# Stage one of a Fourier mixing kernel: two half-width weight tiles in place of two zero-padded full-width ones

## The chip, the cores and the metric

The kernel runs on one core of a Trainium2 chip. A core has a matrix engine (TensorE, PE in the profile; its weight loads are listed apart as PEld), a vector engine (VectorE, DVE), an activation engine (ScalarE, ACT), a general engine (GpSimd, POOL) and a queue engine (SyncE, SP), each with an instruction queue of its own, and 16 DMA engines. The metric is the time of one execution on the device, in microseconds (us); lower is better.

## The reference

The input `x` holds 8 batches of 3072 x 256 numbers. The result is the real part of a Fourier transform over the 3072 positions and the 256 features of each batch, followed by a feed-forward layer that takes the largest of three products:

```python
def _attn_ref(x) -> np.ndarray:
    X = np.fft.fft(x, axis=1)
    X = np.fft.fft(X, axis=2)
    return X.real.astype(np.float32)

def _moe_ref(x, w1, w2, w3, w_out) -> np.ndarray:
    h = np.maximum(np.maximum(x @ w1, x @ w2), x @ w3)
    return (h @ w_out).astype(np.float32)
```

The output is 24576 x 256 in float32.

## The kernel before

The transform over 3072 positions is done as 32 x 96. For each batch a `Mix` object (L358 and on) has these steps: `s(k)` for k = 0 to 6 is stage one, `y` writes its result to DRAM in another order, `z` reads it back into `yb`, `u` and `x0` make the column of feature 0 apart, `c` puts that column into `yb`, `k` is the second stage, which gives the even and odd halves `tE` and `tO`, `v` spreads one row over all partitions, and `end` takes the middle position. The transform over the features is folded into the weights: `gE`, `gO`, `gD` stand for the products of the transform's matrix with w1, w2, w3, and `gw` for the part that passes straight to the output.

Stage one multiplies `x` by a table of 64 columns (32 angles, cosine and sine) over 128 partitions. It has 49 positions `s` of 128 features. Positions of even `s` go to the upper 64 partitions of the result `tb`, those of odd `s` to the lower 64. One call `s(k)` for k under 6 takes eight positions: four even ones as the 512 columns of one matmul, four odd ones as those of another, and both add up in one bank `ps1` of 128 x 512 in float32. The weights of both are 128 columns wide. The tile `tabz` (L93) has 192 columns, of which the middle 64 hold the table and the rest zeros; `tab_at[0]` is its columns 64 to 191 (table, then zeros), `tab_at[1]` its columns 0 to 127 (zeros, then table). So the first matmul writes the even positions to the upper half and zeros to the lower, and the second adds zeros to the upper half and the odd positions to the lower. `s(6)` is the last position alone: one matmul of 128 columns (L375), of which only 64 partitions are read. An eviction (a copy by ACT, in batch 1 for two of them by DVE) then takes the bank to `tb` (L373, L377).

The table itself is made once at the start, by DVE from the sines that ACT gives (L224 to L226).

The main part runs over 8 batches x 18 units (`UNITS`, three blocks of 512 positions x six columns of 128 hidden features). A unit's `begin` and `finish` do the products of the first layer (L437, L438, L445, and for odd units L756, L758, L772, L773, whose third product goes over ACT, DVE and POOL in `third`), and `l2_some` puts ten steps of the second layer (L461, L476, L484) among them. The next batch's `Mix` steps are put between units by a table written out by hand, `ahead` (L729 to L734): the order on each engine's queue is fixed by it.

```python
    ahead = {1: ("s0", "s1"), 2: ("s2", "y0", "s3"), 3: ("u", "s4", "s5"), 4: ("s6", "y1", "x"),
             7: ("z",), 11: ("c",), 12: ("kO0",), 13: ("v0", "kE0", "kO1"), 14: ("v1", "kE1"),
             15: ("kO2",), 16: ("v2", "kE2", "end")}
```

So for batches 2 to 7 PE meets three groups of four stage-one matmuls (units 1, 2 and 3) and then that of `s(6)` alone (unit 4), which `x0` follows (L400): two matmuls with 98 columns of weights that POOL copies in `u` (L395). In batch 0 all is done at the start in two groups (L599 to L608), with idle matmuls (`warm_up`, L589) ahead of each; in batch 1 there are three groups. `ps1` comes from a pool of three banks (`ps_f`, L79) that `k`, `third`, `l2_block` and others share; in batch 0 from one of five (`ps_s`).

In the last batch `l2_mid` (L535) does the middle positions of all batches: among its matmuls are eight whose weights have only 8 columns (L555, L461).

Of the kernel before, what the change touches and what calls it, by code (L numbers as in the profile page):

```python
# [10 lines left out]
BF16 = mybir.dt.bfloat16  # L11
INT32 = mybir.dt.int32
AX = mybir.ActivationFunctionType
ALU = mybir.AluOpType
# [36 lines left out]
def kernel(  # L51
# [9 lines left out]
    nc = tc.nc  # L61
# [16 lines left out]
    consts = ctx.enter_context(tc.tile_pool(name="consts", bufs=1))  # L78
# [11 lines left out]
    x0s = consts.tile([128, RI], BF16, tag="x0s")  # L90
    x0u = consts.tile([128, KS + 1], BF16, tag="x0u")
    ybv = yb.rearrange("p (r e f) -> p r e f", e=2, f=128)
    tabz = consts.tile([128, 192], BF16, tag="tabz")  # L93
    tab_at = [tabz[:, 64:192], tabz[:, 0:128]]
    tabx = consts.tile([128, 2 * RI], BF16, tag="tabx")
    te_tab = consts.tile([128, NHALF + 1], BF16, tag="te_tab")
    to_tab = consts.tile([128, NHALF + 1], BF16, tag="to_tab")
# [20 lines left out]
    def load_x(b, s0, s1, h):  # L118

        rows = x[b].rearrange("(a s) d -> a s d", s=96)  # L120
        lo, hi = (s0, s1) if h == 0 else (max(s0, 1), min(s1, 48))
        src = rows[:, lo:hi, :] if h == 0 else rows[:, 97 - hi:97 - lo, :][:, ::-1, :]
        return nc.gpsimd.dma_start(out=xt[b % 2][32 * h:32 * h + 32, lo:hi, :], in_=src)
# [75 lines left out]
    def small(name):  # L199
        return gen.tile([128, 1], FP32, name=name, tag=name)  # L200

    def scal(out, in0, s1, op0, s2=None, op1=None, eng=None):
        kw = {} if op1 is None else {"op1": op1}
        return (eng or nc.vector).tensor_scalar(out=out, in0=in0, scalar1=s1, scalar2=s2,
                                                op0=op0, **kw)

    up, sidx, hflag, alpha, sig, sgm = (small(n) for n in
                                        ("up", "sidx", "hflag", "alpha", "sig", "sgm"))
# [10 lines left out]
    ang_q = gen.tile([128, 4 * RI], FP32, tag="ang_q")  # L219
# [1 line left out]
                                   op0=ALU.mult, op1=ALU.add)  # L221
    _reduce(nc, ang_r, ang_r, ang_q, 32.0)
    nc.scalar.activation(out=ang_q, in_=ang_r, func=AX.Sin, scale=float(2.0 * math.pi / 32.0))
    nc.vector.memset(tabz, 0.0)  # L224
    nc.vector.tensor_copy(out=tabz[:, 64:128:2], in_=ang_q[:, 0:32])
    scal(tabz[:, 65:128:2], ang_q[:, 0:32], sig, ALU.mult)  # L226
    scal(tabx, ang_q[:, 2 * RI:4 * RI], sgm, ALU.mult)

    dve = nc.vector.tensor_copy
# [8 lines left out]
    for fc in range(2):  # L238
        scal(pf[:, fc:fc + 1], pidx, float(128 * fc), ALU.add)
        nc.vector.scalar_tensor_tensor(  # L240
            out=vm[:, fc * 256:(fc + 1) * 256].rearrange("p (k c) -> p k c", c=128),
# [14 lines left out]
                          in_=par.unsqueeze(1).to_broadcast([128, 2, 2]))  # L256
# [101 lines left out]
    class Mix:  # L358
# [8 lines left out]
        def s(self, k, pool=ps_f, evict=nc.scalar.copy):  # L367
            ps1 = pool.tile([128, 512], FP32, name="ps1", tag="ps")
            if k < 6:
                for hh in range(2):  # L370
                    nc.tensor.matmul(ps1, tab_at[hh], self.x[:, 8 * k + hh:8 * k + 8:2, 0:128],  # L371
                                     start=(hh == 0), stop=(hh == 1))
                evict(out=tb[:, k * 512:(k + 1) * 512], in_=ps1)  # L373
            else:
                nc.tensor.matmul(ps1[:, 0:128], tab_at[0], self.x[:, 48, 0:128],  # L375
                                 start=True, stop=True)
                evict(out=tbv[0:64, 24, :], in_=ps1[0:64, 0:128])  # L377

        def y(self, s0=0, s1=NS, second=nc.sync):
# [241 lines left out]
    for (s0, s1) in HALVES:  # L621
        for h in range(2):
            load_x(1, s0, s1, h)
        if s0 == 0:
            nc.gpsimd.dma_start(out=wout_bf.rearrange("p (jc c) -> p jc c", jc=NJC),
                                in_=moe_w_out.rearrange("(jc p) c -> p jc c", jc=NJC))
# [235 lines left out]
```

## Time and profile before

The median of the runs is 408.67 us. The page and the trace come from one profiled execution with its own time.

| | |
|---|---|
| runs before, us | 408.67, 407.83, 408.88 |
| the profiled execution | 407.28 us |
| its span, first to last instruction | 405.5 us |
| granted TensorE clock, mean | 0.993 |
| matmuls of L371 (512 columns) | 96, 379 ns each from start to modelled end |
| matmuls of L375 (128 columns) | 8, 219 ns each |
| evictions L373 by ACT | 46, 586 ns (median) |
| evictions L373 by DVE | 2, 692 ns |
| evictions L377 by ACT (64 x 128) | 8, 258 ns (median) |

A line of a group names the source line, the engine, the operation, output and inputs with the weights' and the moving tile's sizes, then the count, the busy time in us and the mean in ns of one, and the idle time of the engine just before. A matmul's duration runs to a modelled end, and the next one starts before that: what a matmul costs PE's queue is the distance from its start to the next start, which the timeline shows. A timeline line is the start and the length of a stretch, what ran in it and how many, and in square brackets the idle time before it with what ended it. The chain of waits is followed back from the last instruction, at each step to what released it.

### The profile page before, as it was taken

What the parts mean: (1) busy time and instruction counts of PE and PEld (TensorE: products, weight loads), DVE (VectorE), ACT (ScalarE), POOL (GpSimd) and SP (SyncE); (2) the same over time, 40 slices, a digit from 0 to 9 for tenths busy, and PEclk for the clock granted to TensorE, in tenths of its full rate; (3) what the DMA queues carried; (4) which work ended last, traced back from release to release, by engine and by line L of the source; (5) the groups of instructions that cost most, each with busy time, mean ns of one, the idle gap of its engine ahead of it and who ended that gap; (6) DMA issues with size and microseconds to landing.
All of it is one profiled execution on the core that took longest, in us unless ns stands there. A gap on an engine that the chain in (4) does not pass through costs nothing.

```text
span 405.5 us, 8306 instructions
## 1 busy us (share of the span) xinstructions
PE 388.1 (96%) x2695; PEld 242.7 (60%) x2743; DVE 319.3 (79%) x543; ACT 262.8 (65%) x466; POOL 322.1 (79%) x403
## 2 busy tenths in 40 slices
PE   8689899999999999999999999999999999999995
PEld 3245466656666566656665666656666656666574
DVE  7869787867887887867887887867887887887982
ACT  2565779768866778568875778567875546635430
POOL 7376469878989799888988799887988699788991
PEclk9899999999999999999999999999999999999999
DMA  8999967495765858394765958395532553322225
GB/s 126 195 167 186 187 192 139 127 171 143 162 151 105 178 156 164 107 169 116 188 158 107 180 146 163 114 163 129 150 106 78 145 142 99 96 66 69 88 81 142
DMA packets 69692, 56.30 MB, mean 139 GB/s; under 512 B 35040, under 2 KB 65248, under 8 KB 68452
## 3 DMA queue, kind: packets, MB, share of 16 engines
q0 software_dynamic: 23376, 26.27, 35.0%
q1 hardware_dynamic: 45106, 28.86, 27.3%
q10 hardware_dynamic: 1168, 0.65, 0.6%
q8 instruction: 21, 0.34, 0.3%
q14 instruction: 21, 0.17, 0.2%
HBM read 38.15 MB, written 31.71 MB: 172 GB/s over the span
## 4 chain that ended last, share of the span: by engine, by line
PE 70%; DMA 11%; DVE 5%; issue 4%; ACT 4%; POOL 4%; SPq 1%; ACTq 0%; DVEq 0%; POOLq 0%
PE po L461 24%; PE pse L445 10%; PE pse L437 7%; DMA out_dram<-ot 7%; PE pse L438 5%; PE pse L772 3%; PE po L484 3%; PE d L758 3%; PE pse L773 3%; PE e L756 3%; PE ps L412 2%; DVE even L761 2%; DMA yb<-db 2%; PE pl L476 2%; POOL minus L765 2%
## 5 line engine op out<-in xcount | busy, mean ns | idle before, releaser
L451 ACT ACTIVATE stmp<-pse 128x512 bf16<-128x512 f32 x150 | 89.6, 598 | 61.7 <-PE pse L445 46.4
L765 POOL TENSOR_TENSOR plus<-even,odd 128x512 bf16<-128x512 f32 x69 | 87.9, 1273 | 41.2 <-DVE even L761 35.0
L571 POOL DMA_INDIRECT out_dram<-ot,rows_m x92 | 102.4, 1113 | 17.8 <-issue 9.3
L765 POOL TENSOR_TENSOR minus<-even,odd 128x512 bf16<-128x512 f32 x69 | 87.6, 1270 | 0.0
L774 DVE SCALAR_TENSOR_TENSOR hp<-pse,plus 128x512 bf16<-128x512 f32 x69 | 47.6, 690 | 49.8 <-PE pse L773 21.3
L461 PE MATMUL po<-wout_bf,hp 128*128 128x256 bf16 x576 | 86.1, 273 | 0.3
L461 PE MATMUL po<-wout_bf,hm 128*128 128x256 bf16 x576 | 78.6, 273 | 0.0
L461 PEld LDWEIGHTS <-hp 128*128 128x128 bf16 x576 | 56.3, 98 | 26.1
L445 PE MATMUL pse<-tO,gD 128*128 128x512 bf16 x218 | 70.6, 378 | 0.7
L461 PEld LDWEIGHTS <-hm 128*128 128x128 bf16 x576 | 56.3, 98 | 16.4
L489 DVE TENSOR_TENSOR ot<-po,even 128x512 f32<-128x512 f32 x92 | 62.7, 682 | 0.0
L452 DVE TENSOR_TENSOR hp<-pse,stmp 128x512 bf16<-128x512 f32 x75 | 51.4, 685 | 10.9 <-ACT stmp L451 9.3
L437 PE MATMUL pse<-tE,gE 128*128 128x512 bf16 x147 | 55.6, 378 | 1.5 <-ACT stmp L451 0.2
L452 DVE TENSOR_TENSOR hm<-pse,stmp 128x512 bf16<-128x512 f32 x75 | 51.6, 688 | 6.4 <-ACT stmp L451 2.7
L761 DVE SCALAR_TENSOR_TENSOR even<-vb,wcol,e 128x512 f32<-128x512 bf16 x69 | 50.9, 737 | 0.0
L786 DVE SCALAR_TENSOR_TENSOR hm<-pse,minus 128x512 bf16<-128x512 f32 x69 | 47.1, 682 | 3.6 <-PE pse L445 3.4
L438 PE MATMUL pse<-tO,gO 128*128 128x512 bf16 x130 | 49.2, 379 | 0.6 <-ACT tO L414 0.4
L760 ACT ACTIVATE odd<-d 128x512 f32<-128x512 f32 x69 | 41.3, 598 | 6.7
L130 ACT COPY xt<-xt 64x762 bf16<-64x762 bf16 (+1 forms) x48 | 40.2, 838 | 1.1
L373 ACT CAST tb<-ps 128x512 bf16<-128x512 f32 x46 | 24.8, 589 | 23.2 <-PE ps L371 23.1
L445 PEld LDWEIGHTS <-gD 128*128 128x128 bf16 x219 | 21.2, 97 | 20.3 <-issue 0.7
L484 PE MATMUL po<-gw,tO 128*128 128x512 bf16 x86 | 32.7, 380 | 0.0
(156 smaller groups left out, 475.1 us busy)
## 6 DMA issues: line engine op xcount, KB each, us to landing
yb<-db SPq DMA_DIRECT2D x7, 833.0 KB
xt<-in_x_dram POOLq DMA_DIRECT2D x14, 384.0 KB, 6.2
out_dram<-ot SPq DMA_DIRECT2D x56, 96.0 KB
out_dram<-ot SPq DMA_DIRECT2D x64, 64.0 KB
db<-tb SPq DMA_DIRECT2D x21, 192.0 KB
vb<-vd SPq DMA_DIRECT2D x23, 128.0 KB
xt<-in_x_dram POOLq DMA_DIRECT2D x7, 400.0 KB, 6.1
xt<-in_x_dram POOLq DMA_DIRECT2D x7, 368.0 KB, 5.9
```

The costliest lines, as they stand in the source:

```text
L437: nc.tensor.matmul(pse[:, 0:n], gE[i][:, js], te, start=True, stop=False)
L438: nc.tensor.matmul(pse[:, 0:n], gO[i][:, js], to, start=False, stop=True)
L445: nc.tensor.matmul(pse, gD[i][:, js], to, start=False, stop=True, skip_group_check=True)
L451: nc.scalar.activation(out=stmp[:, 0:n], in_=pses[0][:, 0:n], func=AX.Relu)
L452: nc.vector.tensor_tensor(out=dst, in0=src3, in1=stmp[:, 0:n], op=ALU.max)
L461: nc.tensor.matmul(po, hcols(jc), wout_bf[:, jc * 256:(jc + 1) * 256], start=False, stop=(jc == NJC - 1), skip_group_check=True)
L489: nc.vector.tensor_tensor(out=ot.rearrange("p (h c) -> p h c", h=2), in0=po.rearrange("p (h c) -> p h c", h=2), in1=lin.unsqueeze(1).to_br ...
L571: stored(nc.gpsimd.indirect_dma_start(out, bass.IndirectOffsetOnAxis(ap=rows_m[0:128 - lo, at_row: at_row + 1], axis=0), ot[lo:128, 256:51 ...
L761: nc.vector.scalar_tensor_tensor(out=even3, in0=vb, scalar=wcol[:, jc:jc + 1], in1=e3, op0=ALU.mult, op1=ALU.add)
L765: nc.gpsimd.tensor_tensor(out=dst, in0=even3, in1=odd3, op=op)
L774: nc.vector.scalar_tensor_tensor(out=dst, in0=pse2, scalar=0.0, in1=sums[g][0], op0=ALU.max, op1=ALU.max)
L786: nc.vector.scalar_tensor_tensor(out=dst, in0=pses[0], scalar=0.0, in1=sums.pop(g)[1], op0=ALU.max, op1=ALU.max)
```

## The change

The table loses its zeros. It is now `tab`, 64 columns wide, and each matmul of stage one has 64 columns of weights and an output of 64 partitions: partitions 0 to 63 of the bank for the even positions, at column position 0 of the array, and 64 to 127 for the odd ones, at column position 64. Each of the two is a group of its own (start and stop), since nothing is added up any more. `s(6)` uses column position 0 alone. The evictions are as before. The memset of `tabz` is gone.

```diff
-    tabz = consts.tile([128, 192], BF16, tag="tabz")
-    tab_at = [tabz[:, 64:192], tabz[:, 0:128]]
+    tab = consts.tile([128, 64], BF16, tag="tab")
...
-    nc.vector.memset(tabz, 0.0)
-    nc.vector.tensor_copy(out=tabz[:, 64:128:2], in_=ang_q[:, 0:32])
-    scal(tabz[:, 65:128:2], ang_q[:, 0:32], sig, ALU.mult)
+    nc.vector.tensor_copy(out=tab[:, 0:64:2], in_=ang_q[:, 0:32])
+    scal(tab[:, 1:64:2], ang_q[:, 0:32], sig, ALU.mult)
...
                 for hh in range(2):
-                    nc.tensor.matmul(ps1, tab_at[hh], self.x[:, 8 * k + hh:8 * k + 8:2, 0:128],
-                                     start=(hh == 0), stop=(hh == 1))
+                    nc.tensor.matmul(ps1[hh * 64:hh * 64 + 64], tab,
+                                     self.x[:, 8 * k + hh:8 * k + 8:2, 0:128],
+                                     start=True, stop=True, tile_position=(0, 64 * hh))
                 evict(out=tb[:, k * 512:(k + 1) * 512], in_=ps1)
             else:
-                nc.tensor.matmul(ps1[:, 0:128], tab_at[0], self.x[:, 48, 0:128],
-                                 start=True, stop=True)
+                nc.tensor.matmul(ps1[0:64, 0:128], tab, self.x[:, 48, 0:128],
+                                 start=True, stop=True, tile_position=(0, 0))
                 evict(out=tbv[0:64, 24, :], in_=ps1[0:64, 0:128])
```

## The prediction

> **What bounds the kernel now.** I read the page's busy shares and chain first, then the windows of two whole batches, then the places on TensorE (PE) that the change touches.
>
> ```profile
> PE 388.1 (96%) x2695; PEld 242.7 (60%) x2743; DVE 319.3 (79%) x543; ACT 262.8 (65%) x466; POOL 322.1 (79%) x403
> ...
> PE 70%; DMA 11%; DVE 5%; issue 4%; ACT 4%; POOL 4%; SPq 1%; ACTq 0%; DVEq 0%; POOLq 0%
> ```
> ```profile
> 79.47:125.34 45.87, 45.46 (x320) 28.78 (x324) 36.66 (x58) 33.47 (x58) 39.30 (x48) 1.00 0.68 148
> 125.34:171.20 45.86, 45.45 (x321) 28.79 (x324) 36.58 (x58) 33.47 (x58) 39.56 (x48) 1.00 0.67 149
> ```
>
> The windows' columns are the stretch, its length, then busy time of PE, PEld (weight loads), DVE, ACT, POOL, the granted clock, DMA share and GB/s. In a steady batch of 45.9 us PE is idle for 0.4 us, at full clock; the next, POOL, has some 6 us free. So a microsecond of PE's queue is a microsecond of time there, unless a wait grows in its place.
>
> Stage one takes this, in the groups of PE by line and in one stretch of PE's timeline:
>
> ```profile
> L371 PE MATMUL ps<-xt,tabz 128*128 128x512 bf16 x96 | 24.7, 379 | 2.7 <-DVE xt L132 2.0 <-ACT tE L414 0.6
> ```
> ```profile
> 85.75 1.03 PE L371 MATMUL ps<-xt,tabz 128*128 128x512 bf16 x4
> 86.61 0.38 PE L445 MATMUL pse<-tO,gD 128*128 128x512 bf16 x1
> 86.83 0.38 PE L437 MATMUL pse<-tE,gE 128*128 128x512 bf16 x1
> ```
>
> Four matmuls hold PE's queue from 85.75 to 86.61: 0.86, or 0.216 for each (the 0.38 is from start to a modelled end, and overlaps the next). The 96 cost 20.7 us of queue. In batches 2 to 7 they come in three groups of four (`s0 s1`, `s2 s3`, `s4 s5`), then the lone 128-column matmul of `s6`.
>
> **What the change does to a pair.** Two matmuls of 512 columns, each on half of the array's columns, may stream side by side: the pair then costs 0.216 instead of 0.43. No row of this trace shows two matmuls side by side. The bounds: nothing saved (0.216, the spacing of any two 512-column matmuls here), or 0.216 saved less the wait for the second one's weights. I take the second, since the two share neither columns nor output partitions, and since issue would not stop it: at 355.1 to 355.7, the 24 loads and 8-column matmuls of L544 and L546 follow each other every 0.025 us. TensorEngine Tiling (Array Packing) in the Trainium skill says under Key Properties that such tiles execute independently, in parallel. By that the sum is the forecast below (-2.5); without it, +4.0.
>
> **What it adds: the switch.** The half-width form is a second tiling of the array. The trace has one stretch where PE leaves the full array and comes back, the last batch's middle rows, whose weights have 8 columns:
>
> ```profile
> 359.63 0.82 PE L461 MATMUL po<-wout_bf,hp 128*128 128x256 bf16 x6
> 360.38 0.38 PE L555 MATMUL pom<-gw,t_mid 128*8 128x256 bf16 x2
> 360.60 0.82 PE L461 MATMUL pom<-wout_bf,hmid 128*8 128x256 bf16 x6
> 361.35 0.39 PE L445 MATMUL pse<-tO,gD 128*128 128x512 bf16 x1
> ```
>
> Two 256-column matmuls take 0.22 (360.38 to 360.60), so six from 359.63 end their turn at 360.29; the next starts at 360.38: 0.09 to 0.10 late. The eight narrow ones would end at 361.25; L445 starts at 361.35: again 0.10. The waits view calls both idle times "issue": nothing else ends them. Key Properties of the same page has a rule that speaks against this change: changing the tiling mode drains the engine. The trace agrees, with 0.10 each way.
>
> ```profile
> L555 PEld LDWEIGHTS <-t_mid x2: 82/84/85, 360.4 to 360.4; 128*8 128x8 bf16 x2
> ```
> ```profile
> L400 PEld LDWEIGHTS <-x0u x16: 121/123/125, 14.4 to 318.9; 128*98 128x98 bf16 x16
> ```
>
> A load of 8 columns takes 84 ns, one of 98 columns 123; 64 columns lie between, at 84 + 56 x 39/90 = 108. So the first load after a switch is exposed by 0.02 more than in the row above. The second of a pair starts one load later: the two loads of L400 start 0.05 apart at 98 columns, so 0.03 at 64 (bounds 0 and 0.11, nothing or a whole load).
>
> **A group of four in batches 2 to 7.** Before 0.86. After: 0.10 in, 0.02 load, two pairs at 0.216 plus 0.03, 0.10 out: 0.68. It saves 0.18. With no overlap it is 0.86 + 0.22, a loss of 0.22. It breaks even when each pair overlaps by half.
>
> **The third group and `s6`** stand before another wait:
>
> ```profile
> 87.56 1.27 POOL L765 TENSOR_TENSOR minus<-even,odd 128x512 bf16<-128x512 f32 x1
> 88.78 0.26 POOL L395 COPY x0u<-xt 128x49 bf16<-128x49 bf16 x1
> 88.78 0.22 PE L375 MATMUL ps<-xt,tabz 128*128 128x128 bf16 x1
> 89.09 0.17 PEld L400 LDWEIGHTS <-x0u 128*98 128x98 bf16 x2 [0.32 <-POOL x0u L395]
> ```
>
> PE reaches L375 at 88.78, then waits until 89.09 for POOL's `x0u`, which ends at 89.04. The lone matmul of `s6` needs 0.06, so PE has 0.25 spare. POOL's chain there starts from a `third` issued before `s4`, so what the third group saves does not bring `x0u` forward. After: PE comes 0.18 earlier, pays 0.12 in, 0.06, 0.10 out, and stands at L400 0.10 after the old start of L375, before POOL's 0.31. Group and switch together: nothing. Were that wait gone, they would be +0.22 - 0.18, 0.04 lost per batch. With no overlap PE comes at 0.22 + 0.28 = 0.50, 0.19 later than now.
>
> **Batches 0 and 1.** The chain of waits passes through them in the first 55 us:
>
> ```profile
> 13.96 0.62 PE ps L371 x2
> 14.60 0.58 ACT tb L373
> ...
> 44.81 1.12 PE ps L371 x4
> ...
> 49.24 0.60 PE ps L371 x2
> 49.87 0.59 ACT tb L373
> ```
>
> At 13.96 the last pair ends what ACT waits for; side by side it ends 0.19 earlier, and PE has been in the narrow form since 12.2; the way out lies under the ACT work that follows. At 44.81 and 49.24 a pair saves 0.19 and the way out costs 0.10: 0.09 each. The group at 8.43 stands before a wait for `x`, the one at 39.40 beside ACT's chain: nothing. Sum 0.19 + 0.18 = 0.37.
>
> **The rest.** The dropped memset (0.14 at 4.72 on DVE) ends before the first `x` lands at 7.46, so it is hidden. The program has the same count of PE, ACT, POOL and SP instructions in the same order, and 15 more waits of PE on its own earlier matmuls, each at least 17 matmuls back (two at L298, the rest at L756 and L758): done long before, nothing. ACT reads the same bank with the same shapes; it starts earlier. No DMA or queue is moved.
>
> **Sum.** 12 groups x 0.18 = 2.2 (third groups 0), plus 0.37: 2.5 us less. The profiled execution took 407.28 (span 405.5), so 404.8; it lies 1.4 under the shown median of 408.67, which makes 406.2 in terms of that median, the number I give.
>
> **Rivals.**
> No overlap: the pairs stay in line and only the switches are new. Place: each group of PE's queue; price 0.22; it decides from the point where a pair overlaps less than half. 12 x 0.22 = 2.6, plus 6 x 0.19 = 1.1 at L400, plus some 0.3 in batches 0 and 1: +4.0, 412.6. For it: nothing in the trace shows two streams at once, and PE's starts are in strict line. Against it: nothing here is shared but issue.
> Swallowed: the pairs overlap, but PE comes early to a wait. PE's only regular ones are L400 and L484 on DVE's `ot` (0.2 per batch); DVE is at 80% and POOL at 86% of a batch. If 0.36 per batch ends there: 408.3, no change. Against it: DVE has 9 us free in each batch.
> Loads in line: each 64-column load waits for the matmul before it, 0.11 more for each of 4 matmuls in 18 groups, +8, less what the waits hide: with no overlap some 420. Against it: every load here, the 8-column ones too, starts beside the matmul before it. The page TensorE: Matmul & The Clock Gate of the Trainium skill states in Part 3 that loads overlap matmuls in flight only where the row groups differ; here they don't differ, and the trace already has it otherwise.
> Not what it says: the position is taken but the whole array is used, so neither switch nor overlap: 408.7.
>
> **How the numbers follow.** Forecast 0.58, no overlap 0.25, swallowed 0.12, loads in line 0.03, not what it says 0.02. About 0.3% (1.2 us) is what a measurement of this kernel can tell from no change. Of the forecast 0.03 falls inside that (a switch of 0.15 leaves 0.08 per group, 1.3 in all). Faster 0.58 - 0.03 = 0.55; same 0.12 + 0.02 + 0.03 = 0.17; slower 0.28. The forecast's own range is 404.9 (a switch of 0.05, 0.28 per group) to 407.4 (0.15). The range for 8 in 10 takes in no change and no overlap: 404.8 to 412.8.
>
> **What would show it.** In the changed profile, the two matmuls of a pair start 0.03 apart and pairs 0.22 apart; from the last full-width matmul to the first of the group 0.20 to 0.23 instead of 0.11; a group of four holds the queue for 0.68; L400 still starts behind `x0u`, PE idle there 0.2 or so; batches of 45.5 instead of 45.87. Starts 0.216 apart within a pair would prove me wrong at the largest term; a switch above 0.19 each way would turn the sign with the overlap intact.

## The result, and the profile after

The changed kernel takes 405.28 us (median of 6 runs, 404.69 to 405.88) against 408.06 for the kernel before in the same comparison: ratio 0.9933, 95% interval 0.9915 to 0.9952, 2.8 us less. The profiled execution took 405.21 with a span of 403.4, 2.1 less than before. The windows of two steady batches, with the columns of those shown before:

```profile
80.28:125.76 45.48, 44.97 (x320) 27.91 (x325) 36.33 (x58) 33.19 (x58) 39.32 (x48) 1.00 0.69 149
125.76:171.25 45.49, 44.97 (x321) 27.94 (x326) 36.70 (x58) 33.19 (x58) 39.59 (x48) 1.00 0.68 150
```

A batch takes 45.48 in place of 45.87, 0.39 less, with full clock in both. POOL's busy time is what it was, DVE's is 0.33 less in the one and 0.12 more in the other, and ACT's is 0.28 less, though its evictions take the same 589 ns each (mean). The group by line and PE's timeline at one group of four:

```profile
L369 PE MATMUL ps<-xt,tab 128*64 128x512 bf16 x96 | 15.4, 395 | 4.2 <-DVE xt L131 3.4 <-ACT tE L413 0.6
```
```profile
79.97 0.38 PE L460 MATMUL po<-wout_bf,hp 128*128 128x256 bf16 x2
80.28 0.62 PE L369 MATMUL ps<-xt,tab 128*64 128x512 bf16 x4
80.83 0.39 PE L444 MATMUL pse<-tO,gD 128*128 128x512 bf16 x1
81.06 0.38 PE L436 MATMUL pse<-tE,gE 128*128 128x512 bf16 x1
```

Two 256-column matmuls from 79.97 would leave the queue free at 80.19; the group starts at 80.28, 0.09 late, as at the one switch of the trace before. This idle time ahead of a half-width group is called the way in below, that behind it the way out; the two together are a switch. From there to the next full-width start it is 0.55, where it was 0.86. The single records behind the merged line start at 80.280, 80.283, 80.520 and 80.523: a pair's two matmuls 3 ns apart, the pairs 0.24 apart. That is 0.216 of stream and 0.024 more, the first load, which nothing hides after a switch: the first two matmuls last 403 ns in place of 379. In the first group of batch 0, where the first load (8.295) is done long before `x` lets the matmul start (8.713), that matmul lasts 377 and the next one in its half follows after 0.215. From the matmul ahead to the next full-width start a group now takes 0.758, before 0.972; the next one follows 0.227 later in place of 0.216. Net a group of four saves 0.203.

The wait behind `s(6)`:

```profile
85.77 0.74 DVE L760 SCALAR_TENSOR_TENSOR even<-vb,wcol,e 128x512 f32<-128x512 bf16 x1
86.15 0.62 PE L369 MATMUL ps<-xt,tab 128*64 128x512 bf16 x4
86.66 1.26 POOL L764 TENSOR_TENSOR plus<-even,odd 128x512 bf16<-128x512 f32 x1 [0.56 <-DVE even L760]
87.90 1.25 POOL L764 TENSOR_TENSOR minus<-even,odd 128x512 bf16<-128x512 f32 x1
88.98 0.24 PE L374 MATMUL ps<-xt,tab 128*64 128x128 bf16 x1
89.11 0.26 POOL L394 COPY x0u<-xt 128x49 bf16<-128x49 bf16 x1
89.42 0.26 PE L399 MATMUL psx<-tabx,x0u 128*98 128x17 bf16 x2 [0.20 <-POOL x0u L394]
```

The chain DVE `even`, POOL `plus`, `minus`, `x0u`, PE L399 takes 3.65 us (85.77 to 89.42); before it was 85.45 to 89.09, 3.64. It starts ahead of the third group (86.15), so that group and `s(6)` do not move its end. PE stands at L374 0.44 ahead of L399, before 0.31.

### The profile page after: what moved, and what is told of

It is laid out like the page before. It is cut to its first block, busy times and chain, and to the rows that moved or that the text cites. A ratio compares the mean times of both kernels' runs of the same rounds, so it can differ in the third digit from the quotient of the medians.

```text
span 403.4 us, 8304 instructions
## 1 busy us (share of the span) xinstructions
PE 383.7 (95%) x2695; PEld 236.7 (59%) x2743; DVE 319.6 (79%) x542; ACT 261.2 (65%) x466; POOL 322.1 (80%) x403
## 4 chain that ended last, share of the span: by engine, by line
PE 73%; DMA 9%; DVE 5%; issue 5%; POOL 4%; ACT 3%; SPq 1%; ACTq 0%; DVEq 0%; POOLq 0%
PE po L460 25%; PE pse L444 10%; PE pse L436 7%; DMA out_dram<-ot 6%; PE pse L437 5%; PE pse L771 4%; PE po L483 4%; PE d L757 3%; PE pse L772 3%; PE e L755 3%; DVE even L760 3%; PE ps L411 2%; DMA xt<-in_x_dram 2%; PE pl L475 2%; POOL minus L764 2%
```

## The experiments

All ratios are to the kernel before, with 95% intervals. Behind the first comparison three series were run, each with its own runs of the kernel before (407.97, 407.7 and 407.5 us in the median): control to split_groups, one_column to more_warm, and the rest.

| kernel | us | ratio | interval | steady batch, us |
|---|---|---|---|---|
| before | 408.06 | 1 | | 45.87 |
| changed | 405.28 | 0.9933 | 0.9915 to 0.9952 | 45.48 |
| control (changed again) | 405.9 | 0.9949 | 0.9931 to 0.9968 | 45.48 |
| same_column | 406.85 | 0.9977 | 0.9964 to 0.9990 | 45.70 |
| full_last | 405.85 | 0.9958 | 0.9943 to 0.9973 | 45.48 |
| split_groups | 420.92 | 1.0319 | 1.0294 to 1.0343 | 47.86 |
| one_column | 412.13 | 1.0127 | 1.0088 to 1.0167 | 46.51 |
| split_even | 408.96 | 1.0033 | 1.0010 to 1.0056 | 45.93 |
| x_later_s6_joined | 402.91 | 0.9889 | 0.9855 to 0.9922 | 44.90 |
| more_warm | 405.5 | 0.9953 | 0.9931 to 0.9975 | 45.48 |
| before_x_later | 406.05 | 0.9955 | 0.9940 to 0.9970 | 45.51 |
| x_later | 403.12 | 0.9893 | 0.9872 to 0.9915 | 45.11 |
| warm_all | 405.48 | 0.9944 | 0.9923 to 0.9965 | 45.48 |
| joined_warm_all | 401.95 | 0.9858 | 0.9833 to 0.9883 | 44.90 |

The batch is the distance from one batch's first stage-one group (or L399) to the next's in the profile. It repeats within 0.05 us in most batches and between profiles of equal code, where whole times differ by a few tenths of a per cent, so it carries most of the verdicts. In six of the profiles, those of the kernel before and of the control among them, one or two of the five batches are 0.2 to 0.7 longer; the reason was not traced, and the table gives the others.

**control.** The changed kernel once more, beside the next three.

> The changed kernel again, beside the others on the same chip. Theory: the pairs overlap, a steady group of four holds the queue for 0.76 us from the start of the matmul before it to the next full-width start (0.97 before the change), batches take 45.5 us, ratio to before 0.9933 within 0.002. Rival (the gain is a difference between chips or a lucky draw): a ratio of 0.997 to 1.003. Also looked at: whether TensorE's clock is again granted at half from about 14.2 us after the start (17.8 before the change) until 21; if that is an accident of the first run, it will start at 17.8 here.

The ratio came out at 0.9949, its interval just holding the first series' 0.9933, and the batch at 45.48: the gain is real, 0.5% to 0.7% by the two medians. The clock fell to half at 13.3 us, so the early fall was no accident of the first run; more on it below.

**same_column.** The two calls of a group are issued as column 0, column 0, column 64, column 64.

```diff
-                for hh in range(2):
-                    nc.tensor.matmul(ps1[hh * 64:hh * 64 + 64], tab,
...
+            for hh in range(2):
+                for k, ps1, evict in zip((k1, k2), banks, evicts):
+                    nc.tensor.matmul(ps1[hh * 64:hh * 64 + 64], tab,
+                                     self.x[:, 8 * k + hh:8 * k + 8:2, 0:128],
+                                     start=True, stop=True, tile_position=(0, 64 * hh))
+                    if hh == 1:
+                        evict(out=tb[:, k * 512:(k + 1) * 512], in_=ps1)
```

> In batches 1 to 7 the two calls of a group are issued as column 0, column 0, column 64, column 64, so only the middle two of four can run side by side; loads, widths, switches and work are those of the changed kernel. Theory (the gain is the overlap of different columns): a group takes three slots of 0.216 in place of two, 0.97 from start to start in place of 0.76; 12 groups x 0.21 = 2.5 us above the changed kernel (the third groups are covered by the wait for x0u), about the time before the change, ratio 0.999. Rival (the gain is in the narrower weights, the missing accumulation or something else that doesn't depend on which columns follow each other): the time of the changed kernel, ratio 0.993.

Neither came true. The first two groups of each batch took 0.76, not 0.97; only the third took 0.97. The records of a first group, with the semaphores they wait for or raise, which tell them apart (the second column-0 matmul waits for ACT, the first column-64 one raises PE's by more than one, the last by one):

```
start us  ns   what
79.827    402  column 0 of s0, waits for ACT
79.834    403  column 64 of s0, raises PE's semaphore
80.066    379  column 0 of s1, waits for ACT
80.073    379  column 64 of s1, raises PE's semaphore
```

In the program's order the third of these is the second. The column-64 matmul of `s0` started while `s1`'s column-0 matmul, listed ahead of it, still waited for its half of the array (the bank that it also waits for was free: ACT's last work ahead of this group ended at 79.51). In the third group of the batch, the records are at 85.705, 85.921 (column 64), 85.945 and 86.160: there nothing started beside the first, and the matmul of the other column started 0.22 later, together with the next load of column 0. What held it back shows on ACT, whose copy of `pl` gives a bank back to the pool that `ps1` is taken from:

```profile
85.28 0.59 ACT L489 COPY even<-pl 128x512 f32<-128x512 f32 x1
85.70 0.83 PE L382 MATMUL ps<-xt,tab 128*64 128x512 bf16 x4
```

The copy ends at 85.87, after the group's start, and the column-64 matmul starts 0.05 later; in the next batch the two are at 131.57 and 131.63. So the older matmul held the younger one back while it waited for ACT's signal, and did not while it waited for its half of the array. The batch of 45.70 is 0.22 above the changed kernel for another reason, seen on ACT. In the changed kernel and then in this one, the evictions of a second group (which starts at 83.11 and at 82.66):

```profile
83.56 1.07 ACT L372 CAST tb<-ps 128x512 bf16<-128x512 f32 x2 [1.25 <-PE ps L369]
```
```profile
83.32 1.07 ACT L386 CAST tb<-ps 128x512 bf16<-128x512 f32 x2 [1.26 <-PE ps L382]
```

ACT starts 0.45 after the group's start in the one, 0.66 in the other, although the first bank's matmuls ended equally early: it starts when the matmul listed ahead, that of the second pair (80.066 + 0.379 in the first group), has ended. So the start passed an older matmul, and the signal did not. The late eviction delays ACT's `stmp` behind it and DVE's `hm` and `even` (`even` starts 1.45 after L769's start, in the changed kernel 1.23 after that of L755, the same step), and with them the chain to `x0u`. This experiment did not take the overlap away, and one_column below was made for that.

**full_last.** `s(6)` alone gets 128 columns with zeros again.

```diff
+    tabz = consts.tile([128, 128], BF16, tag="tabz")
+    tab = tabz[:, 0:64]
...
-                nc.tensor.matmul(ps1[0:64, 0:128], tab, self.x[:, 48, 0:128],
-                                 start=True, stop=True, tile_position=(0, 0))
+                nc.tensor.matmul(ps1[:, 0:128], tabz, self.x[:, 48, 0:128],
+                                 start=True, stop=True)
```

> The last position, s(6), gets 128 columns of weights with zeros again, so the lone switch into the narrow form and back in batches 2 to 7 is gone; the pairs are as changed. Theory (the switch beside s(6) and the third group's gain both lie under the wait for POOL's x0u): the L399 start does not move in its batch, no change against the changed kernel within 0.3 us; the wait at L399 is some 0.2 longer. Rival (the lone switch is paid in full): 6 x 0.2 = 1.2 us faster than the changed kernel.

The batch is 45.48 in both, the medians 405.85 and 405.9. Its timeline has the last position without a switch, and L401 no earlier in its batch:

```profile
87.17 0.38 PE L462 MATMUL po<-wout_bf,hp 128*128 128x256 bf16 x2
87.39 0.22 PE L376 MATMUL ps<-xt,tabz 128*128 128x128 bf16 x1
87.92 0.26 PE L401 MATMUL psx<-tabx,x0u 128*98 128x17 bf16 x2 [0.31 <-ACT tb L378]
```

L376 follows at 0.22 without a delay, and from its start to L401 PE takes 0.53 in place of 0.44. The 0.09 more is the way in that is saved; some 0.2 was expected, but the way out is part of the 0.44. The third group starts at 84.66 here, so L401 comes 3.26 later; in the changed kernel 86.15 to 89.42, 3.27. The line names ACT's eviction, which had just ended, but L401 need not wait for it: in the changed kernel L399 starts at 89.42 and that eviction (L376) ends at 89.52. What ends the wait is `x0u` again, which ends 0.05 ahead in both. The lone switch is covered.

**split_groups.** Work of the second layer between the pairs of the first and second group.

```diff
+        elif what[0] == "l":
+            l2_some(3)
...
-    ahead = {1: ("s0", "s1"), 2: ("s2", "y0", "s3"), 3: ("u", "s4", "s5"), 4: ("s6", "y1", "x"),
+    ahead = {1: ("s0", "l", "s1"), 2: ("s2", "y0", "l", "s3"), 3: ("u", "s4", "s5"), 4: ("s6", "y1", "x"),
```

> Between the two pairs of the first and second group of each batch from 2 on, up to three steps of the second layer are done (full width, work that is due soon anyway), so 12 groups pay the way in and out twice. Theory (a way in costs 0.10 + 0.02, a way out 0.10): 12 x 0.22 = 2.6 us above the changed kernel, near the time before; each lone pair then gains next to nothing. Rival (the idle time at a switch is mostly fixed cost that the surrounding work absorbs): less than 0.8 us above the changed kernel.

It lost 15 us, six times what was expected, and not by the switches. The waits of PE, in the control and then here:

```profile
PE psx L399 <- POOL x0u L394: 1.2, 6, 0.2
```
```profile
PE psx L399 <- POOL x0u L394: 8.7, 6, 1.5
```

The three steps were done on top of the unit's ten, so a store of the second layer came due earlier, and from batch 2 on it stands ahead of `x0u` on POOL's queue, where it stood behind it. From the lone matmul of `s(6)` to L399 it is now 1.69 in place of 0.44: 1.25 of the 2.38 that a batch grew. Each lone pair still shows 0.54 from the matmul ahead to the next full-width start (0.65 behind a matmul of 512 columns). The rest was not traced. The edit changed two things at once; split_even is the clean form.

**one_column.** No overlap; widths, counts and switches are kept.

```diff
-                    nc.tensor.matmul(ps1[hh * 64:hh * 64 + 64], tab,
+                    nc.tensor.matmul(ps1[0:64], tab,
...
-                                     start=True, stop=True, tile_position=(0, 64 * hh))
-                evict(out=tb[:, k * 512:(k + 1) * 512], in_=ps1)
+                                     start=True, stop=True, tile_position=(0, 0))
+                evict(out=tb[0:64, k * 512:(k + 1) * 512], in_=ps1[0:64])
```

> Both matmuls of a pair use column position 0 and write the upper 64 partitions, one after the other, so nothing can overlap; width, loads, count and switches are those of the changed kernel. The odd positions of stage one are left out (the second matmul of a pair replaces the first in the bank; the lower half of tb is zeros), and an eviction has 64 partitions in place of 128. Theory (the gain is overlap, the switches are a loss): a group holds the queue for 1.18 us from the start of the matmul before it to the next full-width start, where the changed kernel has 0.76 and the one before 0.97; 12 groups x 0.42 = 5 us above the changed kernel, 2.5 above the one before, ratio 1.005 to 1.009. Rival (half-width matmuls are cheaper by themselves, by less accumulation or shorter loads): a group below 0.97 and a ratio below 1.

```profile
80.04 0.38 PE L461 MATMUL po<-wout_bf,hp 128*128 128x256 bf16 x2
80.35 1.05 PE L370 MATMUL ps<-xt,tab 128*64 128x512 bf16 x4
81.33 0.39 PE L445 MATMUL pse<-tO,gD 128*128 128x512 bf16 x1
```

A group holds the queue for 0.98 from 80.35 to 81.33, and 1.186 from the matmul ahead: expected 1.18. Half-width matmuls are no cheaper by themselves; without overlap the change is a loss. The whole lost more than expected (1.0127, not 1.005 to 1.009), and the batches show why: one grew by 1.03, not 0.84: two groups at 0.43, and of the third only 0.27 was covered by the wait for `x0u` (from `s(6)` to L400 it is 0.17 now, PE no longer waits), which leaves 0.16. Against the kernel before a batch is 0.64 longer, 3.8 us or 0.9% in six. This kernel also needs a memset of `tb`, 1.39 on DVE in batch 0, which reaches its L400 at 15.9 in place of 14.9 in the control; whether that costs the whole anything is not shown, as the first group of batch 2 starts at 80.35, in the control at 80.45.

**split_even.** As split_groups, but three of the unit's ten steps are moved between the pairs, and every other queue keeps its order.

```diff
-        l2_some(10)
+        l2_some(7 if 1 <= b < B - 1 and u in (1, 2) else 10)
```

> Three of the ten steps of the second layer in units 1 and 2 of batches 1 to 6 are done between the two pairs of a group, not ahead of them; all other queues keep their order, so only the switches are doubled in 12 groups. Theory (a switch costs 0.10 + 0.02 in and 0.10 out, with nothing around it to absorb it, as these groups stand ahead of the chain that ends in the wait for x0u): 12 x 0.22 = 2.6 us above the changed kernel, ratio about 0.9995; batches of 45.9. Rival (the engines beside PE set the batch, and PE's switches are absorbed): within 0.8 us of the changed kernel.

```profile
80.17 0.38 PE L483 MATMUL po<-gw,tO 128*128 128x512 bf16 x1
80.48 0.41 PE L369 MATMUL ps<-xt,tab 128*64 128x512 bf16 x2
80.82 0.39 PE L460 MATMUL po<-wout_bf,hp 128*128 128x256 bf16 x2
81.14 0.41 PE L369 MATMUL ps<-xt,tab 128*64 128x512 bf16 x2
81.48 0.39 PE L444 MATMUL pse<-tO,gD 128*128 128x512 bf16 x1
```

A lone pair takes 0.34 from its start to the next full-width one (80.48 to 80.82, 81.14 to 81.48), and the way in stands ahead of it: 0.31 behind the 0.22 of a 512-column matmul, 0.32 for two 256-column ones at 0.12 and 0.11. The batch is 45.93, 0.45 above the changed kernel: two switches at 0.22, as expected. The ratio of 1.0033 is 0.8% above the control's, where 6 x 0.45 us would be 0.7%; the 0.9995 expected was worked out from the first comparison's 0.9933, and the interval does not hold it.

**x_later_s6_joined, before_x_later and x_later.** `x0` a unit later, so that `x0u` is ready; in the joined form, whose edit is shown, `s(6)` also stands behind `s(5)`, while the other two leave it in unit 4.

```diff
-    ahead = {1: ("s0", "s1"), 2: ("s2", "y0", "s3"), 3: ("u", "s4", "s5"), 4: ("s6", "y1", "x"),
-             7: ("z",),
+    ahead = {1: ("s0", "s1"), 2: ("s2", "y0", "s3"), 3: ("u", "s4", "s5", "s6"), 4: ("y1",), 5: ("x",),
+             7: ("z",),
```

> From batch 2 on s(6) stands right behind s(5), so its lone switch is gone, and x0 (L399) a unit later, behind the end of POOL's x0u. Theory (in the changed kernel the third group's gain and the switch beside s(6) are hidden by the wait for x0u, which then ends the batch): PE no longer waits there (0.29 per batch), and the lone switch (0.20) is saved too: batches of 45.0 in place of 45.5, 6 x 0.49 = 2.9 us below the changed kernel, ratio 0.986 to 0.988. Rival (PE would wait for POOL or DVE elsewhere, since the chain over them sets the batch): less than 0.8 us below the changed kernel.

> The kernel before the change, with x0 (L400) one unit later from batch 2 on. Theory (the wait for POOL's x0u ends each steady batch before the change too): PE saves the 0.25 that it idles there, batches of 45.6 in place of 45.87, 1.5 us below the kernel before, ratio 0.9963. Rival (another wait takes its place): ratio 0.999 to 1.001.

> The changed kernel with x0 (L399) one unit later, s(6) where it was. Theory: PE saves the 0.29 that it idles there beyond the switch, batches of 45.2 in place of 45.48, 1.7 us below the changed kernel, ratio 0.990; and the lone switch of s(6), now uncovered, stands open as 0.20 from the matmul ahead to s(6) and 0.15 behind it, which is what the joined form (batches of 44.9) saves more. With its batch set against that of the kernel before with the same move, all of PE's saving is seen without the wait: three groups at 0.20 less a lone switch at 0.20, 0.4 per batch. Rival (the third group's gain goes to another wait): batches of 45.4 or more.

The windows of one batch in the kernel before with the move, in the changed one with it, and in the joined form:

```profile
81.11:126.62 45.51, 45.19 (x321) 28.80 (x325) 36.67 (x58) 33.48 (x58) 39.34 (x48) 1.00 0.70 149
```
```profile
80.34:125.45 45.11, 44.79 (x319) 27.90 (x324) 36.31 (x58) 33.20 (x58) 39.33 (x48) 1.00 0.69 150
```
```profile
80.67:125.57 44.90, 44.58 (x319) 27.88 (x325) 36.38 (x58) 33.07 (x58) 39.34 (x48) 1.00 0.71 151
```

The batches came within 0.1 us of the theory; the joined form's ratio of 0.9889 is a little above the 0.986 to 0.988 expected, which its interval holds. With the wait gone the kernel before needs 45.51 (0.36 less, of which 0.25 was the wait; the rest was not traced) and the changed one 45.11: 0.40 apart, three groups at 0.20 less the lone switch, now open, at 0.21. The lone switch in x_later's timeline:

```profile
88.73 0.38 PE L460 MATMUL po<-wout_bf,hp 128*128 128x256 bf16 x2
89.04 0.24 PE L374 MATMUL ps<-xt,tab 128*64 128x128 bf16 x1
89.22 0.39 PE L771 MATMUL pse<-tE,gE 128*128 128x512 bf16 x1
```

0.31 for two 256-column matmuls and 0.18 behind 128 columns: 0.38 from the last full-width start to the next one (before_x_later: 0.165). Joining `s(6)` to its group takes exactly that off: 44.90.

**more_warm and warm_all.** Idle matmuls in batch 0, where PE waits for `x` and for ACT: more_warm has ten in place of five ahead of `s(2)`, warm_all this:

```diff
-    warm_up(5)
+    warm_up(9)
...
     m.s(3, pool=ps_s)
+    warm_up(5)
...
     m.x0()
+    warm_up(9, ps_s.tile([128, 512], FP32, name="warm2", tag="ps"))
```

> Ten instead of five idle matmuls ahead of s(2) in batch 0, in a stretch where PE waits for x. Theory (stage one at half its length leaves PE so idle between 10.7 and 14.2 us that the clock falls to half one window, 3.4 us, earlier than before the change, and the weight products at L296 take 4.7 in place of 4.1): the clock is granted in full until 17 or later, some 0.5 us below the changed kernel, ratio 0.992. Rival (the earlier fall is where the clock's window happens to lie in the run): no change.

> The changed kernel with idle matmuls in all three stretches of batch 0 in which PE waits: 9 in place of 5 ahead of s(2), 5 ahead of s(4), 9 behind x0. Theory (the clock falls to half for one or two windows of 3.4 us from 13 to 16 us on, since PE is idle most of 10 to 16.7; where PE was busier, with both matmuls of a pair at one column, it never fell): full clock through to the end, the 16 weight products of L296 in 2.7 where the runs so far had 3.7 to 4.8, and 1 to 2 us below the changed kernel, ratio 0.990 to 0.992. Rival (ACT or a DMA then ends that stretch): the clock stays, and less than 0.5 us is won.

more_warm changed no time, and the clock did not hold until 17: it was at half from 15.8 to 22.6, the ratio 0.9953 beside the control's 0.9949. warm_all kept the clock, and the 16 products took 2.64 from the first start to the last, in the control 4.03; yet the time did not move (0.9944). The chain of waits in warm_all shows why:

```profile
15.39 3.85 DMA db<-tb
...
22.46 0.72 POOL w_bf L164
23.18 5.06 DMA w_bf<-in_moe_w_dram
28.29 0.82 PE psg L296 x4
```

At 28.29 PE has waited 1.4 us for the second half of the weights, whose load is issued behind the DMAs of stage one, and what PE won before is given back there: the other 16 products start at 28.29, in the control at 27.85, in the first profile of the changed kernel at 28.36. In that profile's chain the slow products themselves stand on the path (4.68 from 17.09). So the rival holds: with the clock kept, a DMA ends the stretch instead.

**joined_warm_all.** Both edits.

> Both: s(6) beside s(5), x0 a unit later, and the idle matmuls of batch 0. Theory: the two savings add, as one lies in batch 0 and the other from batch 2 on: 1 to 2 us below the joined form, ratio 0.984 to 0.986. Rival: no more than the joined form, 0.989.

401.95, ratio 0.9858: the best of all, 1.4% below the kernel before. Its interval overlaps that of the joined form (0.9889, 0.9855 to 0.9922), and warm_all alone won nothing, so whether the idle matmuls add to it is not shown; the join and the move of `x0` are.

## Why the prediction held, point by point

**The overlap** was the term of the sum that nothing in the trace before could show, and it is there: 3 to 4 ns between the two matmuls of a pair, and without it (one_column) a group costs 0.43 more. Its size was off: the prediction had the second matmul start 0.03 later, behind its own load, and it starts 0.003 later, since the two loads go side by side too (80.278 and 80.281 in the group shown). So a group saves 0.203, not 0.18: 12 groups make 2.4, not 2.2.

**The switch** was read from the last batch's 8-column matmuls, 0.10 each way and 0.02 for the longer load. It is 0.093 + 0.024 in and 0.096 + 0.011 out; split_even pays 0.45 for two more per batch. But for the load, the half-width mode and the narrower one cost the same.

**The third group and `s(6)`** were put at nothing, under the wait for `x0u`. full_last (the switch gone, batch the same) and x_later (the wait gone, both terms there) bear this out. In the batches 2 x 0.203 = 0.41 was to be saved and 0.39 was.

**Batches 0 and 1.** The two pairs of batch 1 gave 0.09 each (1.20 to 1.11 and 2.12 to 2.03 from the matmul ahead to the next full-width one), as worked out. The 0.19 of batch 0 was not there in the first profile: the clock had fallen by then and the pair took as long as before.

```profile
14.37 0.66 PE ps L369 x2
15.04 0.59 ACT tb L372
```

The line before had 0.62 at this place; where the clock was still full (same_column, split_even, more_warm) the two start 3 to 4 ns apart and `s(6)` 0.24 later. Whole profiles can't tell 0.2 here: the first group of batch 2 starts between 78.8 and 80.8 us in the profiles of the changed form whose batch 0 has the changed kernel's idle matmuls, and at 79.5 and 81.1 in the two of the full-width form.

**The sum** was 2.5; measured 2.8 in the first comparison and 2.1 in the second. From the terms as measured it is 2.4 + 0.18 = 2.6: the groups were put 0.3 too low and batch 0, by the first profile, 0.19 too high, and that the two errors nearly cancel is luck. The first two profiles differ by more: from the first group of batch 2 to the end the changed kernel takes 323.1 in place of 326.0, 2.9 less, and it comes to that group 0.8 later. Of the 2.9, two of the longer batches in the profile before make 0.4, so a single pair of profiles doesn't test the sum; the batches do.

**The rivals.** "No overlap" is refuted by the starts; its price, worked out as +4.0, was +4.4 by the medians where it was built (one_column, with the memset in it). "Swallowed" is refuted by the batches. "Loads in line" is refuted by loads that stand beside running matmuls of the same rows (80.306 and 80.310, under matmuls whose stream lasts until 80.52), and "not what it says" by both the switch and the overlap.

## What to carry to other kernels

Half-width weights at two column positions do run two matmuls in the time of one, but each entry into and exit from that mode costs PE some 0.22 us together here: about the 0.216 that one overlapped 512-column pair wins. So gather pairs into groups, and don't leave a lone narrow matmul behind: the same work in one group fewer was worth 0.2 us per batch. Before counting a saving, look for the wait that ends the stretch; here moving one consumer a unit later was worth as much as the change itself.

## What the runs showed of the hardware that was not expected

**Starts out of order.** In same_column a matmul of the free column half started ahead of an older one whose half was busy (79.834 against 80.066), while ACT, which waits for the signal of the matmul that passed, was let go only after the older one had ended (0.66 after the group's start, not 0.45). The Trainium skill's page TensorE: Matmul & The Clock Gate, Part 3, has matmuls in strict order at start and end; the trace differs for the start, and agrees for the signal.

**The clock after a shorter stage.** With stage one at half its length PE is less busy between 10 and 14 us. The windows of batch 0 in the kernel before with `x0` later, and in the changed kernel:

```profile
10.00:14.00 4.00, 2.41 (x11) 0.80 (x9) 3.53 (x9) 1.49 (x4) 3.62 (x8) 1.00 1.27 196
14.00:18.00 4.00, 1.82 (x11) 0.92 (x12) 3.55 (x16) 2.59 (x8) 0.26 (x1) 1.00 1.25 241
```
```profile
10.00:14.00 4.00, 1.36 (x9) 0.38 (x7) 3.04 (x8) 1.36 (x4) 3.62 (x8) 1.00 1.29 198
14.00:18.00 4.00, 1.92 (x8) 0.80 (x9) 3.55 (x16) 2.39 (x6) 0.26 (x1) 0.52 1.21 229
```

PE is busy for 2.41 of the first four microseconds in the one and 1.36 in the other, and the granted clock of the next four is 1.00 and 0.52. In the kernel before itself the two are 2.03 and 0.97. In all nine profiles with overlapping pairs and no idle matmuls but those ahead of each group, the clock fell to half between 12.5 and 15.9 us, for 3.4 to 10.2 us; in the two full-width ones it fell at 17.8 for 3.4 and not at all, and in one_column, whose pairs run in line, it did not fall. With two full-width profiles this is a tendency, and the busy time of this stretch alone doesn't decide it: more_warm has 2.22 there and fell at 15.8, one_column has 1.92 and did not. What sets the moment is open. It cost no time that the runs could show: warm_all kept the clock and took the control's time.
